# Windowed attention with an expert layer: two gate products moved to GpSimd and ScalarE, two splits and the first counts moved back in their queues

## Chip, cores and metric

One core of one Trainium2 chip. The metric is the device time of one execution in microseconds. Engines are called PE (matrix), DVE (vector), ACT (scalar), POOL or GpSimd, and SP, which here only starts transfers.

## What is computed

For 8 batches of 576 rows and 8 heads of 64 columns: attention in which a row sees itself and the 63 rows before it, then a layer that takes the 128 rows of each batch with the largest gate score, puts them through two matrices and adds the result, scaled by a sigmoid, to these rows.

```python
scores = scale * (q @ k.T), with 0 <= row - column < 64, else -1e9
x = softmax(scores) @ v                       # heads side by side: 576 x 512 per batch
s = x @ w_gate
top = the 128 rows with the largest s
out[top] = x[top] + sigmoid(s[top]) * (relu(x[top] @ w1) @ w2)
```

w1 is 512 x 1024, w2 is 1024 x 512. All is float32; in the expert layer each operand is split into a high and a low part, and three products are summed.

## The kernel before, in words

The rows of all batches form 36 tiles of 128 rows; a batch is 4.5 tiles, so batch 0 is tiles 0 to 3 and half of tile 4, batch 1 the rest of tile 4 and tiles 5 to 8. The main loop (L722) has one slot per tile, and each slot issues work of several tiles. The order in each engine's queue is the order of the program: slot n issues

1. loads for tile n+2 on SP (L725), the loads of as many 256 KB pieces of w1 and w2 as the table `PIECES` (L37) names for this slot (L727), and stores of finished tiles;
2. on GpSimd, the splits (`split_w`, L197) of the pieces loaded one slot earlier: a scaled copy into the high part (L200) and a subtraction of two SBUF tiles for the low part (L202);
3. scores of tile n on PE (`attn_scores`, L258, 32 matmuls, two PSUM tiles);
4. steps of the selection of rows marked "P" and "F0";
5. p times v of tile n-2 on PE (`attn_pv`, L304, 64 matmuls), then steps marked "R0";
6. on DVE the maxima of tile n (`attn_max`, L270, 8 instructions that mask, scale, negate and reduce), on ACT the first half of its exponentials (`attn_exp`, L278), the sums of tile n-2 (L314), then steps marked "S0";
7. transposes of the probabilities of tile n-1 on PE (L286) with a copy by ACT (L288), and the second half of the exponentials;
8. on DVE the output of tile n-2 (`attn_out`, L321 and L322) and its gate score (`attn_gate`, L337: one DVE instruction, L230, that multiplies the tile by the gate vector and sums, 512 columns);
9. compares of the selection ("V"), up to 9 matmuls of the expert layer (`step_moe`, L774), and steps marked "E".

Tile n-2 is thus tile 5 in slot 7 and tile 6 in slot 8. Scores of a slot reuse the PSUM tiles of the slot before, so they start once DVE has taken the maxima there.

The selection of a batch (`choose`, L404) runs over several slots: PE transposes the scores of its tiles into rows (L423), DVE compares every row with every other (L439) and keeps counts, PE counts earlier rows with 15 small matmuls (L471, tile "lo" from the pool `ps_t` of two PSUM tiles that the transposes of step 7 use too), DVE forms differences (L480) and selectors (L487), PE turns these into row numbers (L498, "ix"), DVE makes them integers (L502 fx, L504), and GpSimd gathers the 128 rows with an indirect DMA (L506). For batch 0 the counts stand at "P" of slot 8, differences at "S0" of slot 8, and row numbers at "P" and the gather at "F0" of slot 9, behind the splits of that slot in GpSimd's queue. Batch 1's first transposes (tiles 4 to 7) stand at "P" of slot 10.

The expert layer takes the gathered rows in slot 10 at the earliest: PE transposes them (`moe_in`, L528), and `split` (L214) makes a high part on ACT (L219) and a low part on DVE (L220). The first matmuls (L608) follow in slot 11, in threes: high with high, high with low of the weights, low with high. The hidden halves are transposed (`turn`, L580) and split in the same way, that of batch 0 in slots 13 and 14; the second layer (L666) begins in slot 14. From slot 11 to 36 its matmuls fill PE's time between the attention of the slots.

Of the kernel before, what the change touches and what calls it, by code (L numbers as in the profile page):

```python
# [1 line left out]

# [1 line left out]

# [8 lines left out]
F32 = _mybir.dt.float32  # L13
# [3 lines left out]
AF = _mybir.ActivationFunctionType  # L17
ALU = _mybir.AluOpType
# [3 lines left out]
P = 128  # L22
# [11 lines left out]

PIECES = {3: 1, 4: 1, 5: 1, 6: 2, 7: 2, 8: 1} | {n: 2 for n in range(9, 13)}  # L37

CMPS = 2

# [8 lines left out]
def tile_attention_moe(ctx: ExitStack, tc, q, k, v, wg, w1, w2, outs, B, H, S, D, C):  # L49
    nc = tc.nc  # L50
    E = H * D
# [26 lines left out]
    p_h = pool("h", 9)  # L78
# [24 lines left out]
    for opened in (None, 0, 1):  # L103
        m = const.tile([P, 2, W], F32, name=f"mask{len(maskc)}")
        nc.gpsimd.memset(m, 0.0)
        for c in range(2):
            r = slice(c * W, (c + 1) * W)
            nc.gpsimd.affine_select(
                out=m[r, 1, :], in_=m[r, 1, :], pattern=[[-1, W]],
# [3 lines left out]
            else:  # L113
                nc.gpsimd.affine_select(
                    out=m[r, 0, :], in_=m[r, 0, :], pattern=[[1, W]],
# [10 lines left out]
        out=later[:, :P], in_=later[:, :P], pattern=[[1, P]], compare_op=ALU.is_gt,  # L126
# [20 lines left out]
    scores = const.tile([P, NM], F32, name="scores")  # L147
    wgb = const.tile([P, E], F32, name="wgb")
# [65 lines left out]
    def split(ps, hi, lo, n):  # L214

        step = 1 if attended() else n
        for c in range(0, n, step):
            r = slice(c, c + step)
            nc.scalar.copy(hi[:, r], ps[:, r])  # L219
            nc.vector.tensor_tensor(out=lo[:, r], in0=ps[:, r], in1=hi[:, r].bitcast(F32),  # L220
                                    op=ALU.subtract)


    def junk():
        njunk[0] += 1
        return p_jk.tile([P, E], BF16, tag="jk", name=f"jk{njunk[0]}")

    def gate_dot(xf, acc):
        n = acc.shape[0]
        nc.vector.tensor_tensor_reduce(  # L230
            out=junk()[:n, :E], in0=xf[:n], in1=wgb[:n], op0=ALU.mult, op1=ALU.add,
            scale=1.0, scalar=0.0, accum_out=acc)
# [9 lines left out]
    st_x = {}  # L242
# [19 lines left out]
    def attn_max(m):  # L262
        s = st_s.pop(m)
        o = opens(m)
        mk = maskc[0 if o is None else 1 + o]
        pe = p_p.tile([P, NP, 2, 2, W], F32, tag="p", name=f"p{m}")
        nm = p_small.tile([P, 2, NP], F32, tag="nm", name=f"nm{m}")
        for r in range(2):
            for j in range(NP):
                nc.vector.tensor_tensor_reduce(  # L270
                    out=pe[:, j, :, r], in0=s[r][:, j], in1=mk, op0=ALU.add,
                    op1=ALU.min, scale=-SCALE, scalar=3.0e38, accum_out=nm[:, r, j:j + 1])
        st_p[m] = pe, nm

    def attn_exp(m, r):
        pe, nm = st_p[m]
        for j in range(NP):
            nc.scalar.activation(pe[:, j, :, r], pe[:, j, :, r], AF.Exp,  # L278
                                 bias=nm[:, r, j:j + 1], scale=-1.0)
# [55 lines left out]
            nc.sync.dma_start(outs[b + 1][:W, :], xf[W:])  # L335

    def attn_gate(m):  # L337
        gate_dot(st_x[m], scores[:, m:m + 1])

# [2 lines left out]
    slot = 0  # L344
# [59 lines left out]
    def choose(b):  # L404
# [42 lines left out]
        at = "P" if soon else "E"  # L447
# [15 lines left out]
                yield "V"  # L463
        if b == 1:
            soon, at = False, "E"
        yield at

        below = ps_t.tile([P, 512], F32, tag="x", name=f"lo{b}")
        for u in range(NT):
# [12 lines left out]
        for t, (_, r, lo, _) in enumerate(segs):  # L482
            if t == half:
                sel = sel_half[odd]
            else:
                sel = p_sel.tile([P, C], BF16, tag="sel", name=f"sel{b}_{t}")
            (nc.vector if urgent or b in (1, 6) else nc.gpsimd).tensor_scalar(  # L487
                out=sel[r], in0=slots[r], scalar1=diff[r, t:t + 1],
# [8 lines left out]
        for t in range(NT):  # L497
# [9 lines left out]
            out=xe[:C], out_offset=None, in_=outs[b],  # L507
# [214 lines left out]
    for n in range(NM + 3):  # L722
        slot = n
        if n + AHEAD < NM:
            load(n + AHEAD)  # L725
        for _ in range(PIECES.get(n, 0)):
            load_w(loaded)  # L727
            split_at.setdefault(n + 1, []).append(loaded)
            loaded += 1
        for m in range(NM):  # L730
            if m + (4 if m < 5 else 3 if m >= NM - 9 else 6) == n:
                attn_store(m)

        if n in split_at:
            behind_compares()
        for st in split_at.get(n, ()):
            split_w(st)
        step_chain("R")
        step_chain("F")
        step_chain("S")  # L740
        if n < NM:
            attn_scores(n)
        if n in KEEP:
            keep_warm(KEEP[n])
        step_chain("P")
        step_chain("F0")
        if 0 <= n - 2 < NM:
            attn_pv(n - 2)
        step_chain("R0")
        if n < NM:  # L750
            attn_max(n)
            attn_exp(n, 0)
        if 0 <= n - 2 < NM:
            attn_sum(n - 2)
        step_chain("S0")
        if 0 <= n - 1 < NM:
            for a in range(2):
                attn_transpose(n - 1, a)
        if n < NM:
            attn_exp(n, 1)  # L760
        if 0 <= n - 2 < NM:
            attn_out(n - 2)
            attn_gate(n - 2)
            for b in range(B):
                for part, (_, t1) in enumerate(CUT):
                    if SEG[b][t1 - 1][0] == n - 2:
                        closed[b, part] = n
                        if part == 0:
                            c = choose(b)
                            chains[c] = next(c)  # L770
        step_chain("V")
        if n == 0:
            clear()
        step_moe(QUANTA)  # L774
        step_chain("E")
# [45 lines left out]
```

## Time and profile before

| | us |
|---|---|
| median of 3 runs | 250.86 (247.77 to 251.31) |
| the profiled execution | 249.5 |
| its span, first to last instruction | 247.8 |
| PE busy | 228.5 (92%) |
| DVE busy | 182.5 (74%) |
| ACT busy | 155.4 (63%) |
| GpSimd busy | 71.1 (29%) |

Times within the profile count from the span's start. Busy shares are means over stages with different limits. PE's scores of slots 7, 8, 9, 10, 11 and 14 begin at 32.48, 36.58, 43.62, 48.52, 52.98 and 71.47 us; a slot number in the text can be placed by these.

### The profile page before, as it was taken

To read this page: it belongs to the slowest core of one execution; us is meant where nothing else is said; L and a number is where in the kernel's file an instruction comes from. 1 tells how busy PE (TensorE), PEld (TensorE's weight loads), DVE (VectorE), ACT (ScalarE), POOL (GpSimd) and SP (SyncE) were. 2 spreads that over 40 slices of the span, in tenths; PEclk is the share of its full clock that TensorE was granted. 3 is DMA by queue.
4 is the path that set the end of the run, shared out by engine and by line. 5 is a ranking of instruction groups with operands and counts; after the bars stand their busy time and mean duration, and the time that the engine had idled before them with its cause. 6 is when DMAs were issued, how large, how long until landed. Compare 5 with 4: busy or idle time off the path is not lost. (4 is left out here: it accounts for less than half of the span.)

```text
span 247.8 us, 10898 instructions
## 1 busy us (share of the span) xinstructions
PE 228.5 (92%) x4406; PEld 198.4 (80%) x4406; DVE 182.5 (74%) x935; ACT 155.4 (63%) x457; POOL 71.1 (29%) x115
## 2 busy tenths in 40 slices
PE   8886787988898999999899999999999899999991
PEld 7675676777787888988788978888888899899891
DVE  0588899778888889879986898798879995342510
ACT  2997876786776986876878768859878122022100
POOL 7406783492640101014016010530061111110011
PEclk9999998899999999999999999999999999999999
DMA  6999998799566766866877672587212221101011
GB/s 231 389 385 376 329 357 263 252 309 356 183 173 177 218 229 194 276 199 188 256 235 236 189 233 91 168 288 246 74 46 87 109 65 44 42 3 42 0 45 42
DMA packets 25154, 47.26 MB, mean 191 GB/s; under 512 B 2960, under 2 KB 3984, under 8 KB 25104
## 3 DMA queue, kind: packets, MB, share of 16 engines
q1 hardware_dynamic: 23680, 42.10, 51.5%
q0 software_dynamic: 1280, 4.20, 5.3%
q8 instruction: 35, 0.57, 1.0%
q10 hardware_dynamic: 144, 0.26, 0.3%
q14 instruction: 15, 0.12, 0.1%
HBM read 35.01 MB, written 11.53 MB: 188 GB/s over the span
## 5 line engine op out<-in xcount | busy, mean ns | idle before, releaser
L278 ACT ACTIVATE p<-p,nm 128x128 f32<-128x128 f32 x288 | 91.8, 394 | 35.4 <-DVE nm L270 33.0
L270 DVE CUSTOM_DVE_ANT_0 p<-s,mask 128x128 f32<-128x128 f32 x288 | 63.5, 285 | 14.8 <-PE s L258 14.7
L304 PE MATMUL av<-v,pt 64*64 64x65 f32 x2176 | 42.1, 220 | 5.8 <-issue 5.8
L304 PEld LDWEIGHTS av<-v,pt 64*64 64x64 f32 x2176 | 39.1, 134 | 7.4 <-issue 6.3
L258 PE MATMUL s<-k,q 64*64 64x128 f32 x1152 | 41.8, 279 | 2.0 <-DVE nm L270 1.0
L286 PE MATMUL t<-ident,p 128*128 128x128 f32 x288 | 41.0, 284 | 0.9 <-DVE fx L502 0.6
L288 ACT COPY pt<-t 128x512 f32<-128x512 f32 x72 | 38.4, 580 | 3.9 <-PE t L286 3.1
L258 PEld LDWEIGHTS s<-k,q 64*64 64x64 f32 x1152 | 32.5, 135 | 10.2 <-issue 8.3
L286 PEld LDWEIGHTS t<-ident,p 128*128 128x128 f32 x288 | 31.5, 142 | 4.7 <-DVE fx L502 1.3
L230 DVE CUSTOM_DVE_ANT_0 jk<-x,wgb 128x512 bf16<-128x512 f32 x36 | 28.7, 797 | 1.2
L666 PE MATMUL yp<-w2h,hh 128*128 128x512 f32 (+1 forms) x72 | 27.8, 386 | 0.0
L322 DVE TENSOR_TENSOR x<-av,z 128x512 f32<-128x512 f32 x36 | 24.9, 692 | 3.4
L676 POOL DMA_INDIRECT out_dram<-xe,idx x8 | 8.1, 1009 | 67.1 <-DVE xe L671 32.4
L666 PE MATMUL yp<-w2l,hh 128*128 128x512 f32 (+1 forms) x72 | 26.9, 374 | 0.0
L666 PE MATMUL yp<-w2h,hl 128*128 128x512 f32 (+1 forms) x72 | 26.9, 373 | 0.0
L270 DVE DVE_READ_ACCUMULATOR2_ANT nm<- 128x1 f32 x288 | 23.6, 82 | 0.0
L439 DVE SCALAR_TENSOR_TENSOR cmp<-row,scores,later 128x128 bf16<-128x128 f32 (+11 forms) x39 | 19.9, 540 | 0.7 <-ACT row L430 0.5
L506 POOL DMA_INDIRECT xe<-out_dram,idx x8 | 8.3, 1040 | 39.9 <-DVE nm L270 29.5
L487 POOL TENSOR_SCALAR sel<-slots,diff 128x128 bf16<-128x128 f32 x16 | 11.7, 741 | 26.8 <-DVE diff L480 26.4
L625 PE MATMUL hp<-xh,w1h 128*128 128x256 f32 x64 | 18.4, 287 | 0.0
L625 PE MATMUL hp<-xl,w1h 128*128 128x256 f32 x64 | 18.2, 285 | 0.0
L625 PE MATMUL hp<-xh,w1l 128*128 128x256 f32 x64 | 18.1, 282 | 0.0
(88 smaller groups left out, 328.2 us busy)
## 6 DMA issues: line engine op xcount, KB each, us to landing
v<-in_v SPq DMA_DIRECT2D x36, 260.0 KB, 5.1
q<-in_q SPq DMA_DIRECT2D x36, 256.0 KB, 4.7
out_dram<-x SPq DMA_DIRECT2D x32, 256.0 KB, 3.9
k<-in_k SPq DMA_DIRECT2D x31, 256.0 KB, 4.8
st<-in_w SPq DMA_DIRECT2D x16, 256.0 KB, 4.1
k<-in_k SPq DMA_DIRECT2D x8, 128.0 KB
out_dram<-x SPq DMA_DIRECT2D x8, 128.0 KB, 2.7
k<-in_k ACTq DMA_DIRECT2D x1, 256.0 KB
```

The source lines that it names most:

```text
L230: nc.vector.tensor_tensor_reduce(out=junk()[:n, :E], in0=xf[:n], in1=wgb[:n], op0=ALU.mult, op1=ALU.add, scale=1.0, scalar=0.0, accum_out=acc)
L258: nc.tensor.matmul(s[r][c * W:(c + 1) * W, j], Q[m][rs, j, c], keys(m, c, j, rs), start=True, stop=True)
L270: nc.vector.tensor_tensor_reduce(out=pe[:, j, :, r], in0=s[r][:, j], in1=mk, op0=ALU.add, op1=ALU.min, scale=-SCALE, scalar=3.0e38, accum_ ...
L278: nc.scalar.activation(pe[:, j, :, r], pe[:, j, :, r], AF.Exp, bias=nm[:, r, j:j + 1], scale=-1.0)
L286: nc.tensor.transpose(t[:, j, :], pe[:, j, a].rearrange("p r w -> p (r w)"), ident)
L288: nc.scalar.copy(pt, t)
L304: nc.tensor.matmul(av[cs, r, j * D1:(j + 1) * D1], pt[a][rs, j, cs], V[g // 2][rs, g % 2, j], start=a == 0 or o == c, stop=a == 1)
L322: nc.vector.tensor_tensor(out=x.rearrange("p j r d -> p r j d"), in0=av[:, :, :, :D], in1=z[:, 1].unsqueeze(3).to_broadcast([P, 2, NP, D]) ...
L439: nc.vector.scalar_tensor_tensor(out=above[t][r, c0:c1], in0=src[r, c0 - base:c1 - base], scalar=scores[r, m:m + 1], in1=later[r, c0 - a:c ...
L487: (nc.vector if urgent or b in (1, 6) else nc.gpsimd).tensor_scalar(out=sel[r], in0=slots[r], scalar1=diff[r, t:t + 1], scalar2=float(lo - ...
L625: nc.tensor.matmul(hp[:, j], w[:, c, js], a[:, c].rearrange("p u c -> p (u c)"), start=(n == 0), stop=(n == 3 * KC1 - 1))
L666: nc.tensor.matmul(yp[:C, :wide], a[:, c % per, us], w[:, c, es], start=(n == 0), stop=(n == 3 * KC2 - 1))
```

## The change

- `PIECES` names other slots: the first piece is loaded in slot 2, not 3, and split one slot later; slots 7 and 8 split one piece each instead of two, slot 9 two instead of one, slot 13 one instead of two.
- The gate scores of tiles 5 and 6 (`LENT`) are no longer made by DVE: GpSimd multiplies the tile by the gate vector into a float32 tile, and ACT sums it with an Identity activation that stands behind the second half of the next slot's exponentials.
- In `split`, up to slot 13 (`EARLY`) the low part is put into DVE's queue behind the maxima of the next slot, not at once.
- Batch 0's count matmuls move from "P" to "R0", so behind p times v of the same slot.

```diff
-PIECES = {3: 1, 4: 1, 5: 1, 6: 2, 7: 2, 8: 1} | {n: 2 for n in range(9, 13)}
+PIECES = {2: 1, 3: 1, 4: 1, 5: 2, 6: 1, 7: 1, 8: 2, 9: 2, 10: 2, 11: 2, 12: 1}
+LENT = (5, 6)
+EARLY = 13
...
             nc.scalar.copy(hi[:, r], ps[:, r])
-            nc.vector.tensor_tensor(out=lo[:, r], in0=ps[:, r], in1=hi[:, r].bitcast(F32),
-                                    op=ALU.subtract)
+            rest = partial(nc.vector.tensor_tensor, out=lo[:, r], in0=ps[:, r],
+                           in1=hi[:, r].bitcast(F32), op=ALU.subtract)
+            if slot <= EARLY:
+                behind_max.append(rest)
+            else:
+                rest()
...
     def attn_gate(m):
-        gate_dot(st_x[m], scores[:, m:m + 1])
+        if m not in LENT:
+            gate_dot(st_x[m], scores[:, m:m + 1])
+            return
+        prod = p_h.tile([P, E], F32, tag="h", name=f"prod{m}")
+        nc.gpsimd.tensor_tensor(out=prod, in0=st_x[m], in1=wgb, op=ALU.mult)
+        behind_exp.append(partial(nc.scalar.activation, junk(), prod, AF.Identity,
+                                  accum_out=scores[:, m:m + 1]))
...
-        yield at
+        yield "R0" if b == 0 else at
         below = ps_t.tile([P, 512], F32, tag="x", name=f"lo{b}")
...
         if n < NM:
             attn_max(n)
+            flush(behind_max)
             attn_exp(n, 0)
...
         if n < NM:
             attn_exp(n, 1)
+        flush(behind_exp)
```

`flush` calls what its list holds and empties it.

## Rows read from the trace of the kernel before

**Rows 1.** Busy time by stage: stretch, length, engines (instructions), PE's granted clock, DMA share, GB/s

```profile
12.00:36.00 24.00, 19.42 (x567) 16.74 (x567) 20.95 (x113) 19.29 (x59) 13.46 (x14) 1.00 1.02 364
36.00:48.00 12.00, 9.75 (x228) 7.76 (x227) 10.72 (x73) 8.56 (x26) 4.63 (x5) 0.86 0.85 270
...
64.00:186.00 122.00, 119.67 (x2651) 103.29 (x2650) 103.31 (x546) 94.19 (x283) 27.21 (x34) 1.00 0.63 197
```

**Rows 2.** Timeline of PE: start, us, line, operation, tiles, count, idle before and releaser

```profile
22.14 0.81 PE L304 MATMUL av<-v,pt 64*64 64x65 f32 x40 [2.13 <-issue]
...
39.72 0.98 PE L471 MATMUL lo<-oneb,cmp 128*128 128x1 bf16 x5 [0.82 <-DVE cmp L439]
...
43.62 1.83 PE L258 MATMUL s<-k,q 64*64 64x128 f32 x32
...
48.52 1.10 PE L258 MATMUL s<-k,q 64*64 64x128 f32 x32
49.55 0.95 PE L423 MATMUL r<-ident,scores 128*128 128x128 f32 x4
...
52.45 0.60 PE L528 MATMUL xt<-ident,xe 128*128 128x128 f32 x4
...
54.62 0.29 PE L423 MATMUL r<-ident,scores 128*128 128x128 f32 x1 [0.53 <-ACT p L278]
...
56.58 0.57 PE L304 MATMUL av<-v,pt 64*64 64x65 f32 x19 [0.94 <-issue]
...
57.92 0.48 PE L608 MATMUL hp<-w1h,xh 128*128 128x512 f32 x1
...
75.31 0.40 PE L666 MATMUL yp<-w2h,hl 128*128 128x512 f32 x1
```

**Rows 3.** DMA queues of the page: packets, MB, share of 16 engines

```profile
q8 instruction: 35, 0.57, 1.0%
```

**Rows 4.** Busy time from 42 to 44 us, columns as in rows 1

```profile
42.00:44.00 2.00, 2.00 (x16) 1.63 (x19) 1.77 (x11) 0.93 (x3) 0.00 (x0) 0.50 0.69 207
```

**Rows 5.** Timeline of DVE

```profile
18.98 1.81 DVE L230 CUSTOM_DVE_ANT_0 jk<-x,wgb 128x512 bf16<-128x512 f32 x1
...
38.38 0.98 DVE L230 CUSTOM_DVE_ANT_0 jk<-x,wgb 128x512 bf16<-128x512 f32 x1
...
44.45 0.69 DVE L230 CUSTOM_DVE_ANT_0 jk<-x,wgb 128x512 bf16<-128x512 f32 x1
...
45.70 0.16 DVE L502 TENSOR_REDUCE fx<-ix 128x1 f32<-128x2 f32 x1 [0.55 <-PE ix L498]
...
45.97 0.28 DVE L270 CUSTOM_DVE_ANT_0 p<-s,mask 128x128 f32<-128x128 f32 x1
...
71.88 0.69 DVE L220 TENSOR_TENSOR hl<-ht,hh 128x512 fp32r<-128x512 f32 x1 [0.39 <-issue]
...
76.48 0.28 DVE L270 CUSTOM_DVE_ANT_0 p<-s,mask 128x128 f32<-128x128 f32 x1
```

**Rows 6.** Timeline of ACT, second half of slot 9's exponentials

```profile
49.16 1.28 ACT L278 ACTIVATE p<-p,nm 128x128 f32<-128x128 f32 x4
```

**Rows 7.** Groups by form: busy us, mean ns, idle before

```profile
L613 ACT ACTIVATE n<-hp 128x512 f32<-128x512 f32 x8 | 4.7, 590 | 0.0
```

**Rows 8.** Timeline of GpSimd

```profile
18.97 1.27 POOL L202 TENSOR_TENSOR w1l<-st,w1h 128x512 fp32r<-128x512 f32 x1
...
46.35 1.18 POOL L506 DMA_INDIRECT xe<-out_dram,idx  x1 [5.86 <-DVE nm L270]
47.57 0.64 POOL L200 TENSOR_SCALAR w2h<-st 128x512 fp32r<-128x512 f32 x1
...
51.92 0.62 POOL L200 TENSOR_SCALAR w2h<-st 128x512 fp32r<-128x512 f32 x1
```

**Rows 9.** Line 506, the gathers: the first alone (40 to 60 us), then all eight

```profile
DMA to landing us min/median/max: 3.6/3.6/3.6
...
DMA to landing us min/median/max: 3.4/3.7/6.0
```

More of the change, by code (lines that the diff above doesn't have):

```diff
@@ L1 @@
 from contextlib import ExitStack
+from functools import partial
 import numpy as np
@@ L219, in split @@
             nc.scalar.copy(hi[:, r], ps[:, r])
-            nc.vector.tensor_tensor(out=lo[:, r], in0=ps[:, r], in1=hi[:, r].bitcast(F32),
-                                    op=ALU.subtract)
+            rest = partial(nc.vector.tensor_tensor, out=lo[:, r], in0=ps[:, r],
[4 more added lines that the diff above has]
+                rest()
+    behind_max = []
+    behind_exp = []
     def junk():
@@ L337, in attn_gate, with flush @@
     def attn_gate(m):
-        gate_dot(st_x[m], scores[:, m:m + 1])
+        if m not in LENT:
[5 more added lines that the diff above has]
+                                  accum_out=scores[:, m:m + 1]))
+    def flush(todo):
+        for op in todo:
+            op()
+        todo.clear()
     XE = {}
```

## The prediction

> **What bounds the kernel now.** I read the busy times by stage first. From 64 to 186 us PE is busy for 119.67 of 122 us at full clock, so there the time is PE's work and nothing else; before, from 12 to 36 us, PE is busy 19.42 of 24 us while the DMA engines stand at 1.02, and from 36 to 48 us 9.75 of 12 us at a granted clock of 0.86, while DVE is busy 10.72 of 12 [rows 1]. So an edit pays only if PE reaches the start of its dense stretch sooner: the first expert matmul of batch 0 at 57.92 us [rows 2]. From there the order of PE's work is fixed and nearly gapless, so a microsecond gained or lost at that point is one gained or lost at the end.
>
> Second, PE's timeline up to that matmul. Three kinds of gap stand in it. "issue" gaps in the middle of p times v (2.13 us before 22.14, 0.94 before 56.58): the engine waits for no semaphore, the gaps come some 21 of the 64 matmuls later from slot to slot, and they come where the DMA engines are full; PE's program arrives by a queue of its own in 35 packets of some 16 KB [rows 3], so I read them as blocks of instructions that come late. Waits for the counts of batch 0 (0.82 us before 39.72), and a wait for scores at 54.62 (0.53 us). And a half clock: from 42 to 44 us the granted clock is 0.50, the lower of the two levels (1.2 GHz), after the gaps of the slots before; there 32 score matmuls take 1.83 us, and 1.10 us at 48.52 [rows 2, 4].
>
> Third, DVE's timeline from 38 to 46 us: gate of tile 5 (0.98 us at 38.38), compares, maxima of slot 8, differences and selectors, output of tile 6, gate of tile 6 (0.69 us at 44.45), then 0.55 us of waiting for PE's ix, fx, and the maxima of slot 9 at 45.97 [rows 5].
>
> **The change, step by step.** The sum is made against the profiled execution, 249.5 us (span 247.8 us and 1.7 us around it), which is 1.4 us below the median of the runs, 250.86 us, and inside their spread of 247.77 to 251.31 us.
>
> *Gates of tiles 5 and 6 off DVE, counts behind p times v.* Without the gate at 38.38 everything behind it on DVE moves up by some 0.9 us: the compares, maxima of slot 8, differences, and the output of tile 6, which ends at 44.45 - 0.9 = 43.55. PE now runs p times v of slot 8 while the compares finish, so its 0.82 us gap is covered. It doesn't vanish: the second transposed half of slot 8 needs the PSUM buffer of the counts, which DVE frees only with the differences behind the maxima, at about 41.5. Then transposes to 42.0, scores of slot 9 to 43.1 at full clock (43.85 at half), ix 0.25. So fx can start at 43.55 and the maxima of slot 9 at 43.9, or 44.5 at half clock, instead of 45.97. I take 2.05 us gained at this place.
>
> *What ACT gives back.* The score of tile 6 is now the last thing ACT does in slot 9, behind the second half of the exponentials, which ended at 49.16 + 1.28 = 50.44 and now ends at 48.4 [rows 6]. The new activation sums 512 columns; the nearest row is the 128x512 relu, 0.59 us [rows 7]; with a separate accumulator read it may be 0.8, and it can't be below 0.3, a quarter of the 1.28 us that four of 128 columns took [rows 6]. Score at 49.0. The row transposes of batch 1 in slot 10 wait for it; they ended at 50.5 (49.55 in that timeline plus 0.95) and now end at 49.7. The rest of the slot up to the transposes of the gathered rows took 52.45 - 50.5 = 1.95 us [rows 2], so PE comes there at 51.7, 0.75 us earlier than before. Queued behind the new activation on ACT are the row copy and the exponentials of slot 10, which lose 0.6 us by it; that lies beside PE's wait for the gather below, and the maxima that they need come 2 us sooner.
>
> *What GpSimd gives back.* This is the step that I hold decisive. GpSimd's queue is in program order. Before, all splits that stand ahead of batch 0's gather had run long before it: GpSimd sat idle for 5.86 us and sent the gather at 46.35, when DVE gave the indices; two splits followed from 47.57 to 51.92, 2.18 us each on the mean [rows 8]. With the new table the queue holds: split of slot 7, product of tile 5, split of slot 8, product of tile 6, two splits of slot 9, gather. The product of tile 6 waits for the output at 43.55 and takes 1.27 us, like the two-input subtraction of the splits at 18.97 [rows 8]; the splits that the new order keeps behind it take 4.35 us. So the gather goes out at 43.55 + 1.3 + 4.35 = 49.2, although its indices are there at 43.9: 2.85 us later than before, not 2 sooner. From issue to landing the first gather took 3.6 us, all eight 3.4 to 6.0 us with a median of 3.7 [rows 9]; the first ran where DMA was nearly idle, and 49 to 54 us is a full stretch, so I take 4.5: landed at 53.7 (52.6 to 55.2). PE, there at 51.7, waits 2.0 us and transposes at 53.7 instead of 52.45: 1.25 us later.
>
> The Trainium skill, "DMA: Bandwidth & Descriptors", section "Issuing engines are not separate DMA queues", says that transfers started by GpSimd and by SP share the same 16 DMA engines and interleave. By that the gather in a full stretch lands like the slowest row, at 55.2, and the sum below would be 1.5 us higher; the rows bear it out in direction only.
>
> *Slot 11.* The late PE then meets things that are ready: the wait for the score of tile 8 (0.53 us) goes, since DVE has passed it; and the block of instructions has 2 us more to arrive, so its 0.94 us go too [rows 2]. Together -1.47 (at least -0.53). First expert matmul at 57.92 + 1.25 - 1.47 = 57.7: -0.2.
>
> *Early splits.* Only two are issued up to slot 13: that of batch 0's gathered rows in slot 10 and the first hidden half in slot 13. The first lets DVE take the maxima of slot 11 before it waits for ACT; its low part is needed by the third expert matmul, some 0.5 us later than it is made, so it costs nothing, and gains nothing on PE, which is late. The second is worth less than nothing: its low part was made at 71.88, before the maxima of slot 14 (the last at 76.48); behind them, which come 0.8 us sooner without it, it ends at 76.5. The third matmul of the second layer stood at 75.31 and needs it [rows 2, 5]. That is a new stall of 1.2 us; what PE waits for next comes 0.8 us sooner from DVE, so I count +0.4 (0 to 1.2).
>
> *Weight pieces one slot earlier.* The same 16 splits, never later than before against the slot that uses them. They move against the gates: beside GpSimd's subtraction of 1.27 us at 18.97 the gate at 18.98 took 1.81 us, and 0.69 us alone at 44.45 [rows 5, 8]. Re-timed, such a collision may go or another come: -1.1 to +1.1 us on DVE. I take -0.35, a third of it, since with every piece a slot earlier the second split falls about where the first one fell.
>
> The Trainium skill, "GPSIMD Engine Reference", section "Key points", says that GpSimd contends with VectorE instructions that have two SBUF inputs; the trace agrees (1.81 beside 0.69 us). By it the products themselves cost DVE nothing, as what runs beside them reads PSUM, and the two splits pushed to 45 to 49 us would stretch tile 7's gate; that would end by 49.0, with ACT's score.
>
> Sum: -0.2 + 0.4 - 0.35 = -0.15, so 249.4 us. The 2 us gained on DVE are taken back by the gather.
>
> **Rivals.** *The gather is not late* (splits and landing quick, or the product early). For it: a landing of 3.4 us stands in the rows, and indices that are ready early. Against it: program order. Then PE passes at 51.7, 0.75 early, and slot 11 gives 1.47: -0.75 - 1.47 + 0.4 - 0.35 = -2.2, so 247.3 us; with the collision wholly gone and no stall in slot 14, 246.1.
>
> *The late gather brings the half clock back* (slower). For it: PE would idle for 3.5 us in slot 10 if the landing takes 6.0, after gaps in slots 8 to 9, and the granted clock fell after such gaps at 42 us. Against it: 2.13 us of idling at 20 us left the clock at 1.00. It decides from a landing of some 5.5 us: transposes at 55.2, +2.75; slot 11 gives only -0.53; two blocks of PE work at half clock cost 0.73 us each [rows 2]; +0.4: +4.1, so 253.6 us.
>
> *The earlier piece delays PE's instructions.* 256 KB more (0.7 us at the 364 GB/s of rows 1) lie ahead of each block in slots 3 to 5, where DMA is full; the 2.13 us gap could grow by 0.7 in each of one to three slots: 250.1 to 251.5 us. Against it: one piece only, then the table runs level.
>
> **How the numbers follow.** Forecast 0.50, gather not late 0.27, half clock 0.10, late instructions 0.13. 2% of 250.86, 5.0 us, is about what a measurement of this kernel can tell from no change. Faster by more needs 245.8 or less: the first rival at its lower end with one of the instruction gaps closed as well, 0.08. Slower by more needs 255.9: the worst of the second, 0.04. Within 2%: 0.88. The range takes the first rival down to 246.3 and the second up to 253.0.
>
> **What would show it.** Right: batch 0's gather on GpSimd at about 49 us, two splits directly before it, and PE's transposes of gathered rows waiting for its DMA in slot 10; DVE's maxima of slot 9 near 44 us; PE waiting some 1 us for the low part in slot 14; PE busy 98% in between. Wrong: the gather before 47 us, or the first expert matmul earlier than 56.5 or later than 59.5 us.

## The result, and the profile after

The changed kernel takes 252.38 us in the median of 22 runs (249.81 to 255.15), the kernel before 250.61 us on the same chip (22 runs, 246.57 to 261.41). The ratio is 1.0148, interval 1.011 to 1.0186: slower, by less than 2% but well outside the interval. In a later session the unchanged pair gave 1.0084 (1.0047 to 1.0121; medians 251.78 and 249.12 us). The forecast was 249.4 us, 0.15 us less than the profiled execution before; the range of 246.3 to 253.0 us held the median, the direction was missed. All ratios leave out disturbed runs, which matters where many runs of the kernel before were disturbed: the quotient of all runs' medians is 1.0071 for this result and 1.005, 1.004, 1.015 and 1.010 for d1, b_lent, d3 and d4 below, where five or six runs stand against four.

The profiled execution of after took 249.81 us (span 248.1 us), which is the quickest of its 22 runs. So it can't show the loss, and a second trace of the same kernel, f3 (252.92 us, span 251.2 us), is read beside it. First the busy time by stage, columns as in [rows 1], one row of the kernel before:

```profile
48.00:58.00 10.00, 8.45 (x208) 6.97 (x206) 8.02 (x43) 8.80 (x27) 7.96 (x8) 1.00 0.97 314
```

and after:

```profile
12.00:36.00 24.00, 19.75 (x568) 17.00 (x569) 19.98 (x119) 19.66 (x61) 12.49 (x12) 1.00 1.05 375
36.00:48.00 12.00, 9.18 (x262) 7.32 (x262) 10.99 (x76) 11.15 (x35) 8.20 (x8) 1.00 0.97 321
48.00:58.00 10.00, 8.59 (x170) 7.28 (x171) 5.12 (x31) 7.41 (x21) 9.41 (x10) 0.83 0.99 332
...
50.00:52.00 2.00, 2.00 (x16) 1.57 (x8) 1.35 (x3) 1.08 (x3) 1.92 (x3) 0.50 0.96 334
...
64.00:186.00 122.00, 119.12 (x2640) 102.80 (x2640) 101.73 (x539) 92.02 (x278) 24.93 (x31) 0.99 0.63 195
```

The dense stretch is as it was, 119.12 against 119.67 us of PE [rows 1]. GpSimd's work in 36 to 48 us grew from 4.63 to 8.20 us, and in 48 to 58 us, with the DMA engines at 0.99, DVE is busy for 5.12 of 10 us instead of 8.02, and the granted clock is down to 0.83: it is at the lower level (1.2 GHz) from 50 to 52 us, behind a wait of PE that its timeline below shows. The same stretch in f3, and two microseconds of it:

```profile
48.00:58.00 10.00, 5.24 (x111) 4.21 (x111) 3.66 (x21) 5.54 (x17) 9.46 (x10) 0.89 0.91 308
...
56.00:58.00 2.00, 2.00 (x34) 1.67 (x33) 0.01 (x1) 0.59 (x1) 1.92 (x3) 0.50 0.97 363
```

PE is busy for only 5.24 us of 10 there, and at the end of the stretch at the lower level of its clock. GpSimd's timeline of after shows why the gathered rows come late (start, us, engine, line, operation, tiles, in brackets idle before and releaser):

```profile
42.77 1.28 POOL L356 TENSOR_TENSOR prod<-x,wgb 128x512 f32<-128x512 f32 x1 [1.77 <-DVE x L336]
44.01 0.62 POOL L206 TENSOR_SCALAR w1h<-st 128x512 fp32r<-128x512 f32 x1
44.72 1.28 POOL L208 TENSOR_TENSOR w1l<-st,w1h 128x512 fp32r<-128x512 f32 x1
45.96 0.62 POOL L206 TENSOR_SCALAR w2h<-st 128x512 fp32r<-128x512 f32 x1
46.66 1.58 POOL L208 TENSOR_TENSOR w2l<-st,w2h 128x512 fp32r<-128x512 f32 x1
48.42 1.17 POOL L531 DMA_INDIRECT xe<-out_dram,idx  x1 [0.17 <-DVE nm L284]
```

Where the gather stood alone behind 5.86 us of idling [rows 8], it now stands behind the product of tile 6 and two splits without a gap, at 48.42 us instead of 46.35. Its indices were there at 43.1 us. PE's timeline of after, the lines that answer to [rows 2]:

```profile
40.80 0.66 PE L300 MATMUL t<-ident,p 128*128 128x128 f32 x4 [0.54 <-DVE diff L505]
...
48.03 0.43 PE L448 MATMUL r<-ident,scores 128*128 128x128 f32 x2 [1.66 <-ACT jk L362]
48.40 1.79 PE L318 MATMUL av<-v,pt 64*64 64x65 f32 x64
50.12 1.97 PE L300 MATMUL t<-ident,p 128*128 128x128 f32 x8
53.45 0.66 PE L553 MATMUL xt<-ident,xe 128*128 128x128 f32 x4 [1.37 <-DMA xe<-out_dram,idx]
...
57.26 0.48 PE L633 MATMUL hp<-w1h,xh 128*128 128x512 f32 x1
...
75.35 0.50 PE L691 MATMUL yp<-w2h,hh 128*128 128x512 f32 x1 [2.05 <-DVE hl L362]
...
77.55 0.63 PE L691 MATMUL yp<-w2h,hh 128*128 128x512 f32 x1
78.24 1.66 PE L272 MATMUL s<-k,q 64*64 64x128 f32 x32
```

And of f3:

```profile
48.97 0.43 PE L448 MATMUL r<-ident,scores 128*128 128x128 f32 x2 [1.18 <-ACT jk L362]
...
55.31 0.71 PE L553 MATMUL xt<-ident,xe 128*128 128x128 f32 x4 [3.80 <-DMA xe<-out_dram,idx]
55.95 1.99 PE L272 MATMUL s<-k,q 64*64 64x128 f32 x32
...
60.61 0.48 PE L633 MATMUL hp<-w1h,xh 128*128 128x512 f32 x1
...
78.42 0.50 PE L691 MATMUL yp<-w2h,hh 128*128 128x512 f32 x1 [1.78 <-DVE hl L362]
```

Four waits that the rows of before don't have stand in both: the transposed half of slot 8 for DVE's differences, the row transposes of slot 10 for ACT's sum (jk), the gathered rows for the DMA, and the second layer for the low part hl. In f3 PE waits 3.80 us for the gathered rows, and the 32 score matmuls behind them take 1.99 us where 1.10 us is the time at full clock [rows 2]. In after the clock falls earlier, behind the wait of 1.66 us for ACT's sum: p times v then takes 1.79 us and the transposes 1.97 us, against 1.16 and 1.09 us in f3. These 1.5 us cost nothing, as they come out of the wait for the gather, which is 1.37 us there.

**A ledger.** From the starts of PE's scores, each trace can be divided in five: up to slot 1 (its last 30 score matmuls), slots 1 to 9, slots 10 to 13 (where the gathered rows are waited for), slots 14 and 15 (where the low part is), and from slot 16 to the end of the span. Slots 1 to 13 together are called the front. Worked out from the PE timelines, in us; the kernels that haven't been named yet are explained in the experiments:

```
                        to slot 1  1 to 9  10 to 13   14, 15   16 to end   span
before                     7.75     40.77    22.95     11.93     164.40   247.8
after                      7.82     37.04    24.95     14.50     163.79   248.1
f3, after again            7.94     38.22    26.98     14.27     163.79   251.2
e1, low part at once       8.91     37.44    28.16     11.93     164.36   250.8
f2, burden only            8.55     40.44    25.74     12.26     163.71   250.7
d3, sum sooner             8.60     37.66    28.07     13.57     165.20   253.1
b_lent, lent gates alone   8.44     38.29    24.52     12.53     165.12   248.9
d1, one gate lent          7.79     39.89    26.89     13.28     165.15   253.0
f1, relief only            8.91     37.79    22.96     12.07     164.17   245.9
g3, f1 and counts behind   8.58     41.03    22.75     11.93     164.41   248.7
e3, no lent gates          8.49     41.28    22.12     12.37     164.04   248.3
b_early, early splits      8.91     41.11    22.71     14.30     163.77   250.8
e2, gather first           8.73     38.12    24.09     12.46     163.80   247.2
g1, gather first again     8.27     40.31    24.20     13.35     165.27   251.4
g4, no early splits        8.46     40.40    22.27     12.63     165.24   249.0
d4, both sooner            8.70     41.71    23.30     13.20     165.19   252.1
```

f3 against before: +0.2 to slot 1, -2.5 in slots 1 to 9, +4.0 in slots 10 to 13, +2.3 in slots 14 and 15, -0.6 behind, 3.4 us in all. So the time that DVE wins is there when slot 10 begins, and is lost again before slot 14. From slot 16 on nothing moves by more than 0.9 us. The profiled execution of after wins 1.7 us in the front and loses 2.6 us in slots 14 and 15. One trace of each kernel doesn't make a median: those of b_lent and e2, like after's, are the quickest runs of their kernels, that of d1 is the slowest. So the verdicts below are the ratios, and the traces say where.

### The profile page after: what moved, and what is told of

It reads as the page before. It is cut to its first block, busy times and chain, and to the rows that moved or that the text cites. A ratio compares the mean times of both kernels' runs of the same rounds, so it can differ in the third digit from the quotient of the medians.

```text
span 248.1 us, 10903 instructions
## 1 busy us (share of the span) xinstructions
PE 228.7 (92%) x4406; PEld 198.8 (80%) x4406; DVE 178.7 (72%) x931; ACT 155.6 (63%) x461; POOL 73.3 (30%) x117
## 5 line engine op out<-in xcount | busy, mean ns | idle before, releaser
L302 ACT COPY pt<-t 128x512 f32<-128x512 f32 x72 | 38.3, 579 | 3.3 <-PE t L300 3.2
L691 PE MATMUL yp<-w2h,hh 128*128 128x512 f32 (+1 forms) x72 | 28.3, 393 | 2.0 <-DVE hl L362 2.0
L244 DVE CUSTOM_DVE_ANT_0 jk<-x,wgb 128x512 bf16<-128x512 f32 x34 | 24.1, 708 | 1.2
L464 DVE SCALAR_TENSOR_TENSOR cmp<-row,scores,later 128x128 bf16<-128x128 f32 (+11 forms) x39 | 20.9, 566 | 0.7 <-ACT row L455 0.5
L512 POOL TENSOR_SCALAR sel<-slots,diff 128x128 bf16<-128x128 f32 x16 | 11.4, 722 | 26.8 <-DMA k<-in_k 13.9
```

The costliest lines, as they stand in the source:

```text
L244: nc.vector.tensor_tensor_reduce(out=junk()[:n, :E], in0=xf[:n], in1=wgb[:n], op0=ALU.mult, op1=ALU.add, scale=1.0, scalar=0.0, accum_out=acc)
L302: nc.scalar.copy(pt, t)
L464: nc.vector.scalar_tensor_tensor(out=above[t][r, c0:c1], in0=src[r, c0 - base:c1 - base], scalar=scores[r, m:m + 1], in1=later[r, c0 - a:c ...
L691: nc.tensor.matmul(yp[:C, :wide], a[:, c % per, us], w[:, c, es], start=(n == 0), stop=(n == 3 * KC2 - 1))
```

## The experiments

**Which edit costs.** First the parts: the low part of slot 13 at once; the gather ahead of the splits; no lent gates; the early splits alone on the kernel before.

e1, from after:

```diff
-EARLY = 13
+EARLY = 12
```

> The changed kernel, but the low part of slot 13's split (first hidden half of batch 0) is made at once again; the split of slot 10 stays behind the maxima. Theory A (the low part behind the maxima of slot 14 makes PE wait 2.05 us, and the clock falls to half after it, 2.4 us in all at the start of slot 15): some 2.4 us faster than the changed kernel, ratio to the kernel before 0.995 to 1.008, no wait of the second layer's first matmuls for DVE, no half clock near 77 us. Theory B (the late gather with the half clock near 50 us costs the time): no difference to the changed kernel, ratio 1.011 to 1.019, and the microseconds won in slot 14 are waited for elsewhere.

252.53 against 249.45 us, ratio 1.0116 (1.0077 to 1.0155). The wait for hl is gone: PE's timeline of e1 starts the second layer without a bracket, and slots 14 and 15 take 11.93 us as before.

```profile
55.42 1.11 PE L553 MATMUL xt<-ident,xe 128*128 128x128 f32 x4 [3.71 <-DMA xe<-out_dram,idx]
56.46 1.99 PE L272 MATMUL s<-k,q 64*64 64x128 f32 x32
...
77.46 0.60 PE L609 MATMUL ht<-ident,n 128*128 128x128 f32 x4
77.82 0.48 PE L691 MATMUL yp<-w2h,hh 128*128 128x512 f32 x1
```

Yet the kernel is as slow as after, as theory B said. So the low part isn't what makes the difference of the medians; the front still loses 1.9 us against before.

e2, from after, no split between the product of tile 6 and the gather:

```diff
-PIECES = {2: 1, 3: 1, 4: 1, 5: 2, 6: 1, 7: 1, 8: 2, 9: 2, 10: 2, 11: 2, 12: 1}
+PIECES = {2: 1, 3: 1, 4: 1, 5: 2, 6: 1, 7: 1, 9: 3, 10: 2, 11: 2, 12: 2}
```

> The changed kernel with another table of weight pieces: no split in slot 9, so that nothing stands between the product of tile 6 and batch 0's gather in GpSimd's queue; three splits in slot 10. Theory A: the gather goes out at 44 us instead of 48.4 and PE's 1.4 us of waiting for it in slot 10 go, but PE then comes to slot 14 earlier and waits for the same low part longer, so at most 1 us is left at the end, ratio 1.007 to 1.019. Theory B (gather): 1.4 us and one stretch of half clock less, 2 to 3 us faster, ratio 0.995 to 1.007.

252.96 us, ratio 1.0108 (1.0067 to 1.0149). The gather leaves at 45.47 us and lands in 4.6, and PE doesn't wait for it. The median stays slow all the same: a miss for theory B and for any other in which the late gather is the whole loss. Theory A's ratio came true, but not its reason: the wait ahead of the second layer is 1.51 us, shorter than in after. The profiled execution is the quickest of this kernel (248.91 us); g1, below, is a second one.

e3, from after:

```diff
-LENT = (5, 6)
+LENT = ()
```

> The changed kernel with the gates of tiles 5 and 6 back on DVE; early splits, counts behind p times v and the new table stay. Theory A: DVE loses 2 us in slots 7 to 9 and ACT's score no longer delays the row transposes of slot 10 (1.66 us), the gather goes out at its old time or after the two splits that now run before the indices are there; the stall in slot 14 stays: ratio 1.005 to 1.015. Theory C (the product on GpSimd and the sum on ACT are what costs, through the row transposes of slot 10 and the half clock after them): ratio 0.995 to 1.005.

249.64 us, ratio 1.0021 (0.9984 to 1.0058): not told from before, with the new table, the early splits and the counts behind p times v all in place. e1, in the same session, has the lent gates and stands at 1.0116. The loss goes with the lent gates.

b_early, the kernel before with the early splits (`EARLY = 13`) and nothing else:

> The kernel before with the early splits alone (slots 10 and 13 put the low part behind the next maxima). Theory A: PE, which stood at 75.31 us for the low part, waits until about 76.5, and the clock may fall after it: 0.8 to 2.5 us slower, ratio 1.003 to 1.010. Theories B and C: no difference, ratio 0.997 to 1.003.

250.58 us, ratio 1.0033 (0.9989 to 1.0077): PE waits 1.83 us for hl in slot 14 and slots 14 and 15 take 14.30 us in the trace, but the ratio can't be told from 1, and doesn't decide between theory A and the others.

**What of the lent gates costs.** d1 lends tile 5 alone (`LENT = (5,)`); b_lent is the kernel before with the lent gates alone; d3 makes ACT's sum ahead of the second half of the exponentials; d4 is d3 with the table of e2.

```diff
+        flush(behind_exp)
         if n < NM:
             attn_exp(n, 1)
-        flush(behind_exp)
```

> The changed kernel with tile 5 alone lent; tile 6's gate is back on DVE. Tile 5's score is made in slot 8, two slots ahead of the row transposes that need it, and its product stands in GpSimd's queue before the indices are due, so the gather goes out with the indices, some 45 to 46 us. Theory C (it is the second product that costs: the gather behind it and the row transposes behind ACT's score): ratio 0.996 to 1.004, as without any lent tile. Rival (any product on GpSimd and sum on ACT costs, half each): 1.005 to 1.010.

252.63 against 251.40 us (6 runs), 1.014 (1.0075 to 1.0205). PE doesn't wait for the gather, which left at 47.04 us; there is a gap of 2.71 us with nothing waited for in slot 12. It is slower than both theories said. On DVE something new stands: GpSimd's splits, pushed back by the product of tile 5, run beside the four selectors (L512), which take 2.28 us where they take 0.87 us in before; what it costs at the end wasn't tested.

> The kernel before with the two lent gates alone; its own table leaves one split, not two, between the product of tile 6 and the gather, so the gather goes out about 2 us sooner than in the changed kernel (46 to 47 us, where it was). Theory G (the lateness of the gather is what costs): ratio 0.998 to 1.004. Theory R (the row transposes of slot 10 wait for ACT's score, 1.2 to 1.7 us, and the clock falls after it): 1.006 to 1.014, and that wait stands in the trace.

252.36 against 251.40 us (6 runs), 1.0136 (1.0048 to 1.0223): by the ratio the lent gates alone, on the old table, bring the loss; by the medians it is 0.4%, so this kernel is weak evidence. The gather leaves at 48.05 us, later than expected, in part because here too the selectors take 2.27 us; it lands 6.8 us later, and PE waits 3.04 us.

> The changed kernel with ACT's sum of the lent tiles ahead of the second half of the exponentials, not behind it; the gather stays behind two splits. The score of tile 6 is there 1.2 us sooner, about when DVE's score of tile 7 is, so the row transposes of slot 10 wait less than 0.4 us for ACT. Theory R: ratio 0.998 to 1.006. Theory G: PE comes to the gathered rows sooner and waits for them as much longer: 1.010 to 1.018, no difference to the changed kernel.

255.15 us (6 runs), 1.0253 (1.0185 to 1.032), above what either theory gave. PE's timeline of d3:

```profile
48.14 0.62 PE L448 MATMUL r<-ident,scores 128*128 128x128 f32 x2 [0.24 <-ACT jk L362]
...
55.86 1.11 PE L553 MATMUL xt<-ident,xe 128*128 128x128 f32 x4 [4.99 <-DMA xe<-out_dram,idx]
56.90 1.99 PE L272 MATMUL s<-k,q 64*64 64x128 f32 x32
```

The wait for ACT's sum falls to 0.24 us, and what PE saves there it waits longer at the gather, 4.99 us. That ACT's sum sets the end of slot 10 falls with this: the gather ends last.

> Both: ACT's sum ahead of the second half of the exponentials, and no split between the product of tile 6 and the gather. If the two waits together are the cost of the lent gates (theories G and R as two ends of one delay), this is as fast as the changed kernel without lent tiles or faster, ratio 0.990 to 1.002, with the low part of slot 14 as the one new wait that is left. If it stays at 1.008 or more, the cost of the lent gates lies elsewhere (GpSimd beside DVE, or the half clock after other gaps).

254.02 us (6 runs), 1.0163 (1.0053 to 1.0272), a miss for the two waits as the whole cost. No wait for the gather (issued at 47.46, landed in 3.5), none for ACT's sum, and still not quick: 2.18 us of gap with nothing waited for in slot 9, with the clock at 0.50 from 48 to 50 us behind it, and 1.77 us at 57.62 for a gate score of DVE.

**Relief or burden.** The lent gates do two things: they let DVE reach the maxima sooner, and they put work on GpSimd and ACT. f1 has the first alone: from before, DVE keeps the gates of tiles 5 and 6 but does them behind the next slot's maxima. f2 has the second alone: DVE keeps its gates where they were, and GpSimd and ACT make the same sums once more into a column that nobody reads.

```diff
-        prod = p_h.tile([P, E], F32, tag="h", name=f"prod{m}")
-        nc.gpsimd.tensor_tensor(out=prod, in0=st_x[m], in1=wgb, op=ALU.mult)
-        behind_exp.append(partial(nc.scalar.activation, junk(), prod, AF.Identity,
-                                  accum_out=scores[:, m:m + 1]))
+        behind_max.append(partial(gate_dot, st_x[m], scores[:, m:m + 1]))
```

> The kernel before, with the gates of tiles 5 and 6 still whole on DVE, but each behind the maxima of the next slot: DVE is relieved in slots 7 and 8 as by the lent gates, and nothing is added to GpSimd or ACT, so the gather goes out with its indices and the row transposes of slot 10 find their scores. Theory I (what costs is that PE, relieved, runs into what isn't there yet: blocks of instructions and half clock): as slow as the lent gates, ratio 1.006 to 1.014. Theory P (what costs is the added work on GpSimd and ACT and the order behind it): ratio 0.992 to 1.002.

248.95 against 249.12 us, 0.998 (0.9942 to 1.0018). PE's timeline of f1:

```profile
49.47 0.32 PE L445 MATMUL r<-ident,scores 128*128 128x128 f32 x1 [1.03 <-DVE scores L244]
...
51.75 0.60 PE L550 MATMUL xt<-ident,xe 128*128 128x128 f32 x4
...
56.67 0.48 PE L630 MATMUL hp<-w1h,xh 128*128 128x512 f32 x1
```

The gather leaves at 45.34 us, lands in 4.8, and PE passes slot 10 at 51.75 without waiting for it. The sooner maxima harm nothing and, by the ratio, gain nothing that can be told, though this trace, a quick one (247.65 us), is 3.0 us ahead of before in slots 1 to 9.

```diff
+        gate_dot(st_x[m], scores[:, m:m + 1])
         prod = p_h.tile([P, E], F32, tag="h", name=f"prod{m}")
         nc.gpsimd.tensor_tensor(out=prod, in0=st_x[m], in1=wgb, op=ALU.mult)
+        spare = p_small.tile([P, 1], F32, tag="spare", name=f"spare{m}")
         behind_exp.append(partial(nc.scalar.activation, junk(), prod, AF.Identity,
-                                  accum_out=scores[:, m:m + 1]))
+                                  accum_out=spare))
```

> The kernel before with the products on GpSimd and the sums on ACT added, into a column that nobody reads, while DVE makes the gates of tiles 5 and 6 as before: the burden of the lent gates without the relief. Theory P: the gather goes out at some 49 us, PE waits for it in slot 10, ratio 1.006 to 1.016. Theory I: ratio 0.998 to 1.004, since PE comes no sooner.

251.90 against 249.12 us (6 runs), 1.0123 (1.0073 to 1.0172): the burden alone brings a loss as large as that of the change. GpSimd's timeline of f2:

```profile
46.13 1.79 POOL L357 TENSOR_TENSOR prod<-x,wgb 128x512 f32<-128x512 f32 x1 [1.45 <-DVE x L336]
47.88 0.61 POOL L206 TENSOR_SCALAR w1h<-st 128x512 fp32r<-128x512 f32 x1
48.58 1.27 POOL L208 TENSOR_TENSOR w1l<-st,w1h 128x512 fp32r<-128x512 f32 x1
50.03 1.17 POOL L533 DMA_INDIRECT xe<-out_dram,idx  x1 [0.18 <-DVE x L336]
```

and PE's:

```profile
56.92 0.96 PE L555 MATMUL xt<-ident,xe 128*128 128x128 f32 x4 [3.54 <-DMA xe<-out_dram,idx]
57.81 1.99 PE L272 MATMUL s<-k,q 64*64 64x128 f32 x32
```

The gather is out at 50.03 us, lands 6.8 us later, and the scores behind the wait run at half clock. Counted from slot 1, f2 is 0.3 us ahead of before at slot 10, and loses 2.8 us from there to slot 14, where the wait stands. Between f1 and f2 the front of the ledger differs by 5.4 us, in slots 1 to 9 and 10 to 13 by about the same; the medians differ by 2.95 us.

The gather of f2 is later than the order of GpSimd's queue alone makes it. DVE's timelines of before and of f2:

```profile
42.46 0.87 DVE L487 TENSOR_SCALAR sel<-slots,diff 128x128 bf16<-128x128 f32 x4
```

```profile
42.72 2.24 DVE L514 TENSOR_SCALAR sel<-slots,diff 128x128 bf16<-128x128 f32 x4
...
46.08 0.69 DVE L244 CUSTOM_DVE_ANT_0 jk<-x,wgb 128x512 bf16<-128x512 f32 x1
```

Beside the selectors f2 has a split on GpSimd (42.66 to 44.68 us) that the product of tile 5 has pushed back; in before and f1 GpSimd is idle then. That is a second way in which the burden costs time, of 1.4 us, in f2, b_lent and d1. In after and f3 the selectors take 0.88 and 0.89 us, so there it isn't the cause.

> The changed kernel, nothing edited, on the chip of the two others, for a second trace of it: its first trace is of its fastest run. Ratio 1.008 to 1.019. If the landing of the first gather takes 5 us or more, PE waits 2.5 us or more for it in slot 10 and the clock falls to half after it (theory G); if it takes under 4 us, the time must be lost elsewhere.

After unchanged: 251.78 us (11 runs), 1.0084 (1.0047 to 1.0121); its trace stands in the result.

**What is left when the gather goes first.** g1 is e2 once more (one run), g4 is e2 without early splits (`EARLY = -1`), g3 is f1 with the counts behind p times v.

> The changed kernel with no split in slot 9, nothing else edited, for a second trace: the first was of its fastest run (248.9 us), the median was 252.96. Theory I2 (with the gather early, PE in slots 9 and 12 outruns its blocks of instructions): issue gaps of 1.3 us or more in slot 9 and of 1 to 3 us in slot 12, no wait for the gather. Theory H (the half clock after the wait for ACT's score in slot 10 and for the low part in slot 14): issue gaps as in the kernel before (under 1 us), and two stretches at half clock.

253.08 us in one run, before 249.95 in the median. PE's timeline of g1:

```profile
44.48 0.32 PE L272 MATMUL s<-k,q 64*64 64x128 f32 x1 [1.36 <-issue]
...
51.17 0.43 PE L448 MATMUL r<-ident,scores 128*128 128x128 f32 x2 [0.58 <-ACT jk L362]
...
55.87 0.29 PE L448 MATMUL r<-ident,scores 128*128 128x128 f32 x1 [0.69 <-DVE scores L244]
...
64.20 0.34 PE L318 MATMUL av<-v,pt 64*64 64x65 f32 x5 [1.89 <-issue]
```

No wait for the gather; gaps of 1.36 and 1.89 us in slots 9 and 12 in which PE waits for nothing shown, and the waits for scores. The gap in slot 9 is 1.09 to 2.18 us in the five traces with this table or with one lent gate (e2, g1, g4, d1, d4); in f3 it is 0.54 us, in after there is none. In all of them it stands before the last of the slot's 32 score matmuls. In g1, g4 and d4 the granted clock falls behind it (0.57 from 48 to 50 us in g1, 0.50 in g4 and d4), in e2 and d1 it doesn't. Behind it the eight transposes take 2.23 us in g1, 1.09 in f3. In the ledger g1, g4 and d4 take 40.3 to 41.7 us in slots 1 to 9, where after, f3, e1, d3, b_lent and e2 take 37.0 to 38.3: the gain of the relief is gone there.

> The changed kernel with no split in slot 9 and without any early split (low parts made at once): of the new waits only that of the row transposes for ACT's score is left. If the low part of slot 14 and the half clock after it are what the gather-first kernel loses (theory H), ratio 0.996 to 1.005; if it is the instruction blocks (theory I2), 1.006 to 1.014, as with the early splits.

251.75 against 249.95 us, 1.006 (1.0016 to 1.0104), on the border of the two theories. It lies 0.5% under e2's ratio, but the two are from different sessions and their intervals overlap, so that the early splits cost this much is not shown.

> A version that may beat both kernels: the kernel before, gates of tiles 5 and 6 whole on DVE behind the next maxima (the relief alone had ratio 0.998) and batch 0's counts behind p times v, as in the changed kernel. PE's wait for the compares in slot 8 (0.5 to 0.8 us) is covered: 0.990 to 0.998 if that counts at the end, 0.997 to 1.002 if the second transposed half of the slot waits for the differences instead.

249.63 us, 0.9983 (0.9944 to 1.0022). No version beats the kernel before by more than its interval.

## Why the prediction was wrong

**The order of GpSimd's queue: right.** The decisive step said that the product of tile 6 and two splits would stand ahead of the gather, out at 49.2 us. It was at 48.42 us in after, 49.22 in f3, with 1.28 us for the product (1.3 taken) and the two splits directly ahead. Maxima of slot 9 on DVE began at 43.00 us in after and 44.41 in f3 (43.9 taken), and up to slot 10 PE was 3.7 and 2.5 us ahead (2.05 taken). ACT's sum took 0.62 us and a read of 0.20 us, 0.72 in all with their overlap, inside the 0.59 to 0.8 given. Slot 11 lost both its gaps, as said: no bracket stands between the gathered rows and the first expert matmul in after or f3.

**The landing: the step that failed.** "49 to 54 us is a full stretch, so I take 4.5: landed at 53.7". Measured: issue of batch 0's gather, its time to landing, the mean share of the DMA engines in the 3.5 us after the issue, and PE's wait for it, in us:

```
              issued   landing   DMA share   PE's wait
f1            45.34      4.8       0.94        none
e2            45.47      4.6       0.71        none
g1            45.70      3.6       0.64        none
g4            45.89      3.6       0.72        none
before        46.35      3.6       0.58        none
e3            46.70      4.8       0.80        none
g3            46.90      4.0       0.91        none
d1            47.04      5.7       0.73        none
d4            47.46      3.5       0.56        none
b_lent        48.05      6.8       0.92        3.04
after         48.42      5.0       1.00        1.37
b_early       48.66      5.2       0.92        none
f3            49.22      6.1       0.94        3.80
e1            49.47      5.9       1.01        3.71
d3            49.68      6.1       0.98        4.99
f2            50.03      6.8       0.96        3.54
```

Issued between 48 and 50 us it takes 5.0 to 6.8 us, a median of 6.1, where 4.5 was taken from a row of 3.6 and a slowest of 6.0 [rows 9]. The row of 3.6 us was read as one "where DMA was nearly idle"; its share is 0.58, so even that landing had traffic beside it. f3 has 6.1 us, PE's transposes at 55.31 instead of 53.7, and 252.92 us: this is the rival that had a chance of 0.10, "It decides from a landing of some 5.5 us: transposes at 55.2", and 253.6 us in all.

The quickest run of after landed at 53.4 us, the forecast's 53.7, and its first expert matmul stood at 57.26 (57.7 forecast). That agreement is in part luck: the issue was 0.8 us sooner and the landing 0.5 us longer than taken. So is that of the whole execution, 249.81 against 249.4 us: its front was 1.7 us shorter than before and not 0.55, slots 14 and 15 were 2.6 us longer and not 0.4, and 0.6 us were won behind them.

The Trainium skill, "DMA: Bandwidth & Descriptors", section "Issuing engines are not separate DMA queues", has GpSimd's transfers interleave with SP's on the same 16 engines. The prediction worked out 55.2 us by that rule and set it aside; f3 agrees with it (55.31, DMA share 0.91 from 48 to 58 us), after with its 53.45 us doesn't.

**The half clock: its price was known, its chance was not.** After the wait the granted clock is 0.50 (1.2 GHz) from 56 to 58 us in f3 and from 56 to 60 us in e1. The argument against it was that 2.13 us of idling at 20 us had left the clock at 1.00. Here PE waits 3.5 to 5.0 us, in f3 and e1 after a wait of 1.18 us in the same slot, and in e1, f2, f3 and d3 alike the scores that follow take 1.99 us. In b_lent, with 3.04 us, the clock held. In after it fell behind the wait of 1.66 us for ACT's sum. Before has a stretch at half clock as well, at 42 to 44 us [rows 4]; f3 has none there (1.00 from 40 to 54 us), and has it behind the late gather instead.

**The early split of slot 13: the term of +0.4.** The forecast said a stall of 1.2 us at the third matmul, 0.8 of it returned. The wait is 2.05 us in after and 1.78 in f3, and it stands at the first matmul of the second layer, not the third, 0.55 us sooner. Behind it the granted clock fell to 0.50 (76 to 78 us in after), so the first seven matmuls took 2.83 us (75.35 to 78.18) where before they took 1.89 (74.76 to 76.65, the first and the last of them here):

```profile
74.76 0.48 PE L666 MATMUL yp<-w2h,hh 128*128 128x512 f32 x1
...
76.25 0.40 PE L666 MATMUL yp<-w2h,hh 128*128 128x512 f32 x1
```

Slots 14 and 15 took 14.3 to 14.5 us instead of 11.9: +2.3 to +2.6, in two traces. Where the clock held it was +0.4 and +0.5 in e3 and e2 (waits of 1.41 and 1.51 us), the size forecast, and +1.3 to +1.6 in d1, d4, g1 and d3 (1.41 to 1.69 us, with a further gap of 0.4 us in slot 15 in which PE waits for nothing shown). Kernels without the early split of slot 13 have 0 to +0.7 there, so a trace alone doesn't separate +0.4 from nothing. By the ratios the step weighs less than in after and f3: b_early 1.0033 (not told from none), and e1, without it, as slow as after.

**Counts behind p times v.** Said: the 0.82 us gap "doesn't vanish", the transposed half then waits for the differences. It does, for 0.54 us in after and up to 1.33 in g3; g3 (0.9983) beside f1 (0.998) shows no gain.

**Weight pieces and collisions.** In after the gates ran nearly undisturbed: 34 of them at a mean of 0.708 us against 0.797 before, the longest 0.96 instead of 1.81 us. In f3 the mean is 0.756 and the longest 1.48 us, so the -0.35 had some ground; but from slot 1 to slot 7 PE won only 0.2 to 0.7 us (24.57 us in f3 and 24.07 in after against 24.73). That late instructions would delay slots 3 to 5 is excluded by the same numbers.

**The sum.** Forecast: -0.55 us in the front (-0.2 and -0.35), +0.4 in slot 14, -0.15 in all. In f3 the front is +1.5, slots 14 and 15 are +2.3, the rest -0.6: the gain on DVE was there, and two terms of the loss were each some 2 us too small: the landing (6.1 us for 4.5) and the low part, in both of them partly by a half clock that the sum had left out. That half clock was priced in the second rival, whose +4.1 leaves out the -0.35 that the forecast and the first rival count.

**What stays open.** Shown is that the loss comes with the lent gates (e3 beside e1), and from the work they put on GpSimd and ACT, not from DVE's relief (f1, f2). That the late gather is the way it takes in after, f3, e1, d3, b_lent and f2 is what the traces show: slots 10 to 13 take 24.5 to 28.2 us there, and 22.1 to 23.0 us in before and the kernels without lent gates. But taking the delay away (e2, g1, g4, d4) didn't give the whole time back: then a gap without a shown cause in slot 9, a half clock behind it and waits for scores in slots 10 and 11 take the place of the gain. Whether those come from the three splits that e2 packs behind the gather, from their loads, or from what PE meets when it comes sooner wasn't separated, so the late landing is the step of the sum that failed, and not shown to be the only cost of the lent gates. Why PE waits for the low part at the first matmul isn't shown by any row.

## What to carry to other kernels

An in-order queue that ends in a transfer on the critical path is a path itself: work moved "to an idle engine" is paid for when it stands ahead of that transfer, even if the engine is idle 70% of the span. Price a moved transfer at the load of the moment it is moved to, and if the sum is a small difference of a gain and a loss, ask first how far that one landing can spread. When the profiled execution is the quickest run of its kernel, take another trace before explaining the median.

## What the runs showed of the hardware that was not expected

The same 128-row gather landed in 3.5 to 5.7 us in the six traces in which the DMA engines' share was 0.56 to 0.73 in the 3.5 us after its issue, and in 4.0 to 6.8 us in the ten in which it was 0.80 to 1.01. So the share tells the direction, and a single landing still spreads by nearly 3 us.

PE's wait ahead of the second layer left the granted clock at 1.00 in e3, d1, d4, g1, e2 and d3 (1.41 to 1.69 us), and was followed by 0.50 in f3, b_early and after (1.78, 1.83 and 2.05 us); the same half clock stood behind the wait for the gather in e1, f2, f3 and d3 (3.5 to 5.0 us), and not in b_lent (3.04 us). In slot 9 a gap of 1.36 us was followed by it in g1 and not in e2 and d1. So the length of one wait doesn't tell whether the clock falls.

When GpSimd's two-input product and DVE's gate ran side by side, the product was slowed: 1.79 us at 46.13 in f2 beside a gate of 0.69 us at 46.08, while in before it was the gate (1.81 us at 18.98 beside a subtraction of 1.27 us at 18.97 [rows 5, 8]). In both rows the one that started first ran undisturbed. The Trainium skill, "GPSIMD Engine Reference", section "Key points", names contention with VectorE instructions of two SBUF inputs; both pairs agree with it. DVE's selectors were slowed too, from 0.87 us for four in before to 2.24, 2.27 and 2.28 us beside GpSimd's splits in f2, b_lent and d1.
